# Block attention before two expert layers on one Trainium2 core: the first four attention steps laid out, paired and loaded in another way

## The chip, the core and the metric

The kernel runs on one core of a Trainium2 chip. The metric is the device time of one execution in microseconds (us); lower is better. Before the change three runs took 448.31, 448.86 and 450.56 us, median 448.86 us.

## What is computed

Three layers follow one another: causal attention with a decay over blocks of 64 positions (batch 2, 8 heads, 768 positions, head dimension 64), then `leaky(x @ w_in) @ w_out`, then a second expert layer with softmax and layer norm. Only the first is touched by the change:

```python
for b in range(nb):                                   # 12 blocks of 64 positions
    intra = np.einsum('bhic,bhjc->bhij', qb, kb) * Dmask[None]
    intra = np.einsum('bhij,bhjd->bhid', intra, vb)
    inter = np.einsum('bhid,bhde->bhie', qb * lam_pow[None], kv_state)
    out[:, :, sl] = intra + inter
    kb_dec = kb * rev_pow[None]
    kv_state = lam_block[None, :, None, None] * kv_state + np.einsum('bhsd,bhse->bhde', kb_dec, vb)
```

The result, 1536 tokens of 512 values, is the `x` of `h = x @ w_in` (512 to 2048), `g @ w_out` (2048 to 512) and so on.

## The kernel before

**Attention.** One step `s` (0 to 11) is one block of 64 positions, for both batches (`b`) and four pairs of heads (`pr`); the two heads of a pair (`h`) take the two halves of the 128 partitions. Each product is a matmul of a 64x64 stationary and a 64x64 moving operand, so it uses one quarter of the TensorE array: the half of the partitions that its operands lie on, and the half that its result goes to. Two products can lie beside each other in time where they use different quarters. A step has four groups of 16 matmuls (8 for each of the halves):

- `scores_mm` (L192): k times q. `scores_ev` (L198, VectorE) multiplies by the decay mask into `r`.
- `xs_mm` (L238): v times `r`, the part inside the block.
- `state_mm` (L206): decayed k times v. `scale_k` (L172) first multiplies k by its decay (ScalarE, four instructions); `state_ev` (L214) adds the old state, decayed by GpSimd (`decay_state`, L182), on VectorE.
- `xq_mm` (L250): state times scaled q (`scale_q`, L159, GpSimd), added in PSUM to the result of `xs_mm`.

`alone` issues a group by itself, `both` alternates two groups matmul by matmul. Each group is two batches, so `alone` is 32 instructions of 64x64 and `both` 64. The finished step is split into a high and a low part: `x_hi` (L287, ScalarE), then `x_lo` (L291, VectorE).

Steps 0 to 3 stand in a prologue written out by hand (L595 to L642). Steps 4 to 11 are sewn into the loop over the first expert layer. The two kinds have different layouts. From step 4 on, the operands of `xs_mm` and `state_mm` lie turned: the head that `q` has in the upper half has its `v` there too (`rows`, `jrows`). In steps 0 to 3 `v` and the third copy of k lie the other way round, so that `scores_mm` and `xq_mm` use the same two quarters and stand alone, and `xq_mm` writes with other rows of the array than `xs_mm`: a wait for the state's addition (L262) keeps them apart.

**Loads.** Nearly all go through the queue of SyncE (SPq) in program order, by `load` (L113). It adds a wait: a load is issued only when no more than `AHEAD` bytes, itself included, are under way. Beside this, the loads use eight counters in turn, so that a load also waits for the one eight before it. Step loads: `load_step` (L127), for one step two of 384 KB (q, k and k again, of one batch) and one of 256 KB (v). `load_kv` (L152) loads the turned operands of a later step in four of 128 KB, each for 64 partitions. `load_weights(n)` loads weight pair `n`, 512 KB for `IN` and 512 KB for `OUT`. The order is: table, step 0, pair 0, step 1, a copy of the mask, steps 2 and 3, pairs 1 to 3, step 4, pair 4, q and k of step 5, pair 5, and so on.

**Mask.** `scan(dfirst, 0, None)` makes the decay mask with four scans on VectorE; the turned mask `dmask` for steps 4 on is copied from it by two DMAs (L579).

**First expert layer.** The weights come as 64-bit words and are turned into two float parts: `words` (ScalarE, L336 and L337), `clamp`, `shift`, `join` (VectorE, L343, L353, L362), `high` (ScalarE, L392), `low` (VectorE, L411). `l1_mm((0, 0))` (L422) is the first product of the expert layer. It needs the high parts of all four steps. From there TensorE follows the order `l1_mm`, `l2_mm`, ..., 12 matmuls of 128x512 each (L422, L438).

## Time and profile before

| | |
|---|---|
| median of three runs | 448.86 us (448.31 to 450.56) |
| profiled execution, its own time | 449.68 us |
| span of its instructions | 447.9 us |
| TensorE busy | 434.0 us, 97% of the span |
| VectorE / ScalarE / GpSimd busy | 266.5 / 194.9 / 33.0 us |
| chain that ended last | TensorE 84%, DMA 8%, ScalarE 3%, VectorE 2% |

The profile's times are from the span's start; a TensorE instruction's time is its own, and neighbours overlap. [...] The DMA share is the mean busy share of 16 DMA engines. The landing time of a load runs from its issue to its completion.

### The profile page before, as it was taken

The page shows a single profiled execution, that of the slowest core. Times are in us where ns is not written, and L with a number is a line of the kernel's source. Part 1 is how long each engine was busy: PE and PEld are TensorE (multiplying, and loading weights), DVE is VectorE, ACT ScalarE, POOL GpSimd, SP SyncE. Part 2 cuts the span into 40 slices and gives each one's busy share as a digit, 9 for nine tenths or more (in the row PEclk, how much of TensorE's full clock was granted, in tenths as well). Part 3 has the DMA queues.
Part 4 walks back from the last instruction along what each step waited for, and adds up shares of the span by engine and source line. Part 5 has one row for each costly group of instructions (what it writes and reads, how often), then busy time and mean ns, then how long its engine had stood idle before and what let it go on. Part 6 is the DMA issues. An engine that isn't in the chain of part 4 may idle for free.

```text
span 447.9 us, 7951 instructions
## 1 busy us (share of the span) xinstructions
PE 434.0 (97%) x3252; PEld 358.2 (80%) x3252; DVE 266.5 (60%) x411; ACT 194.9 (44%) x326; POOL 33.0 (7%) x39
## 2 busy tenths in 40 slices
PE   6879899999999999999999999999999999999996
PEld 3868688888788888888888888888888888888886
DVE  3479898998932121211131788817779877777640
ACT  3477977868443232121233678622423322222221
POOL 0502022020102020100000000000000000000000
PEclk9699999999999999999999999999999999999999
DMA  7888875951303030100015653000112322222111
GB/s 264 253 282 265 288 273 153 320 194 50 94 0 97 1 95 1 48 0 1 1 23 184 225 198 122 1 0 5 44 34 58 98 72 74 74 75 74 58 48 47
DMA packets 23859, 46.98 MB, mean 105 GB/s; under 512 B 4368, under 2 KB 12176, under 8 KB 23312
## 3 DMA queue, kind: packets, MB, share of 16 engines
q1 hardware_dynamic: 21952, 44.92, 30.4%
q10 hardware_dynamic: 1872, 1.58, 1.2%
q8 instruction: 25, 0.41, 0.4%
q14 instruction: 10, 0.08, 0.1%
HBM read 37.95 MB, written 3.15 MB: 92 GB/s over the span
## 4 chain that ended last, share of the span: by engine, by line
PE 84%; DMA 8%; ACT 3%; DVE 2%; issue 1%; SPq 1%; ACTq 0%
PE acc L438 25%; PE hps L422 25%; PE acc L550 15%; PE aps L458 6%; PE hps L458 5%; PE acc L458 4%; DMA ldw<-in_att_dram 3%; DMA raww<-in_w_out_dram 2%; PE aps L242 1%; DMA qk<-in_att_dram 1%; PE aps L254 1%; PE acc L560 1%; DMA raww<-in_w_in_dram 1%; DMA kv<-in_vt_dram 1%; ACT x L336 1%; ACT raww L337 1%
## 5 line engine op out<-in xcount | busy, mean ns | idle before, releaser
L422 PE MATMUL hps<-xhi,wio 128*128 128x512 f32 x384 | 102.9, 390 | 3.1 <-ACT wio L392 2.4
L429 DVE TENSOR_TENSOR glo<-hps,ghi 128x512 fp32r<-128x512 f32 x48 | 33.2, 691 | 116.2 <-ACT ghi L428 115.8
L438 PE MATMUL acc<-ghi,wio 128*128 128x512 f32 x384 | 96.2, 393 | 0.1
L422 PEld LDWEIGHTS hps<-xhi,wio 128*128 128x128 f32 x384 | 71.7, 188 | 19.1 <-ACT wio L392 3.4
L438 PEld LDWEIGHTS acc<-ghi,wio 128*128 128x128 f32 x384 | 71.3, 188 | 15.6 <-ACT ghi L428 0.5
L425 ACT ACTIVATE hps<-hps 128x512 f32<-128x512 f32 x48 | 28.0, 583 | 116.6 <-PE hps L422 116.6
L550 PE MATMUL acc<-wb,ln 128*128 128x512 f32 (+1 forms) x312 | 67.6, 373 | 0.0
L550 PEld LDWEIGHTS acc<-wb,ln 128*128 128x128 f32 x312 | 55.3, 188 | 10.2
L422 PE MATMUL hps<-xlo,wio 128*128 128x512 f32 x192 | 51.4, 389 | 0.0
L438 PE MATMUL acc<-glo,wio 128*128 128x512 f32 x192 | 51.3, 389 | 0.0
L422 PEld LDWEIGHTS hps<-xlo,wio 128*128 128x128 f32 x192 | 36.0, 188 | 7.6
L438 PEld LDWEIGHTS acc<-glo,wio 128*128 128x128 f32 x192 | 36.0, 188 | 7.5
L353 DVE SCALAR_TENSOR_TENSOR raww<-x,raww 128x1024 uint32<-128x1024 uint32 (+1 forms) x27 | 31.2, 1154 | 0.5
L336 ACT ACTIVATE x<-raww 128x1024 f32<-128x1024 f32 (+1 forms) x27 | 27.7, 1027 | 7.5 <-DMA raww<-in_w_in_dram 5.2
L362 DVE SCALAR_TENSOR_TENSOR x<-x,raww 128x1024 uint32<-128x1024 uint32 (+1 forms) x27 | 29.6, 1096 | 0.8
L428 ACT CAST ghi<-hps 128x512 fp32r<-128x512 f32 x48 | 28.2, 587 | 1.5
L337 ACT ACTIVATE raww<-raww 128x1024 uint32<-128x1024 uint16 (+1 forms) x27 | 27.9, 1033 | 0.0
L491 POOL TENSOR_TENSOR small<-small,nhalf 128x1 f32<-128x1 f32 x12 | 6.6, 550 | 234.5 <-DVE small L490 234.5
L411 DVE TENSOR_TENSOR wio<-x,wio 128x1024 fp32r<-128x1024 f32 (+1 forms) x20 | 22.2, 1111 | 0.6 <-ACT wio L392 0.5
L553 ACT COPY osb<-acc 128x512 f32<-128x512 f32 (+1 forms) x13 | 7.2, 554 | 32.3 <-PE acc L550 19.2
L165 POOL TENSOR_TENSOR qk<-qk,qpow 128x512 f32<-128x512 f32 x8 | 11.3, 1406 | 135.4 <-PE hps L196 135.4
L458 PE MATMUL aps<-wa,xhi 128*128 128x512 f32 x80 | 19.8, 389 | 0.0
(96 smaller groups left out, 494.6 us busy)
## 6 DMA issues: line engine op xcount, KB each, us to landing
raww<-in_w_out_dram SPq DMA_DIRECT2D x23, 512.0 KB, 4.3
raww<-in_w_in_dram SPq DMA_DIRECT2D x16, 512.0 KB, 5.1
qk<-in_att_dram SPq DMA_DIRECT2D x8, 512.0 KB, 4.1
raww<-in_w_in_dram SPq DMA_DIRECT2D x4, 1024.0 KB, 4.8
lt<-e SPq DMA_DIRECT2D x124, 32.0 KB, 1.8
out_dram<-osb SPq DMA_DIRECT2D x11, 256.0 KB, 2.2
ldw<-in_att_dram SPq DMA_DIRECT2D x7, 384.0 KB, 5.1
kv<-in_att_dram SPq DMA_DIRECT2D x16, 128.0 KB, 3.2
```

What stands on the lines that cost most here:

```text
L336: act.activation(x, raw[:, :, 1].bitcast(F32), AF.Copy, scale=HI_SCALE)
L337: act.activation(raw[:, :, 0], raw.bitcast(U16)[:, :, 1], AF.Copy, scale=LO_SCALE)
L353: dve.scalar_tensor_tensor(raw[:, :, 0], x.bitcast(U32), 3, raw[:, :, 0], op0=ALU.logical_shift_left, op1=ALU.bitwise_or)
L362: dve.scalar_tensor_tensor(xu, xu, 0x80000000, raw[:, :, 0], op0=ALU.bitwise_and, op1=ALU.bitwise_or)
L411: dve.tensor_tensor(t[:, 1, halves], x[:, halves], t[:, 0, halves].bitcast(F32), op=ALU.subtract)
L422: pe.matmul(bank, w[:, s, k], x[b][:, k], start=(i == 0), stop=(i == len(terms) - 1))
L425: act.activation(bank, bank, AF.Prelu, alpha=0.01)
L428: act.copy(ghi, bank)
L429: dve.tensor_tensor(glo, bank, ghi.bitcast(F32), op=ALU.subtract)
L438: pe.matmul(acc[m], w[:, s, m], g, start=(f == 0 and first), stop=(f == NF - 1 and last))
L458: pe.matmul(bank, x[b][:, k, o : o + P], w2_t["a", k, half][:, s], start=(i == 0), stop=(i == len(terms) - 1),)
L550: pe.matmul(po[:, 0:n], x[:, k], w2_t["b", k][:, s, cols], start=(i == 0), stop=(i == len(terms) - 1))
```

## The change

Steps 0 to 3 take the layout of the later steps. Their q and k come in two loads of 256 KB, their v and the turned k in four loads of 128 KB with 64 partitions each. Those of step 0 are issued from ScalarE's queue, all others from SyncE's. `scores_mm` now uses the other two quarters than `xq_mm`, and the prologue alternates `xq_mm` of step s with `scores_mm` of step s + 1. In step 3 `xq_mm` comes first and `xs_mm` adds to it. The manual wait is gone. `dmask` is scanned directly, with no `dfirst` and no copy by DMA. `AHEAD` is 2 MB in place of 1.5 MB. The work on the weights in the prologue is in a slightly other order.

```diff
-AHEAD = 3 << 19
+AHEAD = 1 << 21
...
-    def load_step(s):
+    def load_turned(s, kj, v, queue=None):
+        queue = queue or sync
+        for h in range(2):
+            load(queue, out=v[rows(h)], in_=vt[s, HALF[h]])
+        for h in range(2):
+            load(queue, out=kj[rows(h)], in_=att[2 * s : 2 * s + 2, HALF[h], 2].rearrange("n p a b -> p n a b"))
+
+    def load_first_qk(s, queues):
         t = wp.tile([P, 2048], F32, tag="w", name="ldw")
-        qkk = t[:, 0:1536].rearrange("p (n c a b) -> p n c a b", n=NB, c=3, a=NPAIR)
-        v = t[:, 1536:2048].rearrange("p (n a b) -> p n a b", n=NB, a=NPAIR)
+        qk = qk_t[s] = t[:, 0:1024].rearrange("p (n c a b) -> p n c a b", n=NB, c=2, a=NPAIR)
+        kv = kv_t[s] = t[:, 1024:2048].rearrange("p (c n a b) -> p c n a b", c=2, n=NB, a=NPAIR)
         for b in range(NB):
-            load(act if s + b == 1 and s == 0 else sync, out=qkk[:, b], in_=att[2 * s + b])
-        load(sync, out=v, in_=vt[s])
+            load(queues[b], out=qk[:, b], in_=att[2 * s + b, :, 0:2])
...
-            pe.matmul(at(bank, jrows(s, h), b, pr), k[d, b, pr], q[d, b, pr], start=True, stop=True)
+            pe.matmul(at(bank, rows(h), b, pr), k[d, b, pr], q[d, b, pr], start=True, stop=True)
...
-            if s < NPRE and pr + b + h == 0:
-                tc.add_manual_dep(ins, added[s].name, SYNC, reason="another half of rows")
...
-    scan(dfirst, 0, None)
-    load_step(0)
+    load_first_qk(0, (act, sync))
+    load_first_kv(0, act)
     load_weights(0)
-    load_step(1)
-    for h in range(2):
-        load(sync, out=dmask[rows(h)], in_=dfirst[HALF[h]])
-    load_step(2)
-    load_step(3)
+    load_first_qk(1, (sync, sync))
+    load_first_kv(1)
...
     load_weights(1, IN)
     load_weights(1, OUT)
...
-    alone(scores_mm, 2, sb[0])
     state_ev(1, kb)
     decay_state(2, pool)
-    alone(xq_mm, 1, xb[1])
+    both(xq_mm, 1, xb[1], scores_mm, 2, sb[0])
     scores_ev(2, sb[0])
-    join(0)
     x_hi(1, xb[1])
+    high(0)
     both(xs_mm, 2, xb[0], state_mm, 2, kb)
     x_lo(1, xb[1])
     scale_q(3, pool)
     scale_k(3, act)
-    high(0)
-
-    alone(scores_mm, 3, sb[1])
     state_ev(2, kb)
     decay_state(3, pool)
-    alone(xq_mm, 2, xb[0])
+    low(0)
+    both(xq_mm, 2, xb[0], scores_mm, 3, sb[1])
     scores_ev(3, sb[1])
+    alone(xq_mm, 3, xb[1])
+    x_hi(2, xb[0])
     both(xs_mm, 3, xb[1], state_mm, 3, kb)
-    x_hi(2, xb[0])
-    state_ev(3, kb)
-    low(0)
-    alone(xq_mm, 3, xb[1])
     x_lo(2, xb[0])
     words(1, IN)
     x_hi(3, xb[1])
     bits(1, IN)
     x_lo(3, xb[1])
+    state_ev(3, kb)
     words(1, OUT)
```

The instructions of SyncE's queue around the end of the step loads, before. `DMAHW` with a number is one of the eight counters; `ldw` is a step's tile, `raww` a weight pair.

```order
L118 DMA ldw<-in_att_dram 128x768 [waits DMAHW7_49]
L118 DMA ldw<-in_att_dram 128x768 [waits DMAHW2_49]
L118 DMA ldw<-in_vt_dram 128x512 [waits DMAHW3_49]
L118 DMA raww<-in_w_in_dram 128x1024 [waits DMAHW4_49,DMAHW0_49]
L118 DMA raww<-in_w_out_dram 128x1024 [waits DMAHW6_49,DMAHW1_49]
L118 DMA raww<-in_w_in_dram 128x1024 [waits DMAHW7_49]
```

The same place with the change: step 3 (the first six rows), then pairs 1, 2 and the first half of 3.

```order
L109 DMA ldw<-in_att_dram 128x512 [waits DMAHW4_49]
L109 DMA ldw<-in_att_dram 128x512 [waits DMAHW5_49]
L109 DMA ldw<-in_vt_dram 64x512 [waits DMAHW6_49]
L109 DMA ldw<-in_vt_dram 64x512 [waits DMAHW7_49]
L109 DMA ldw<-in_att_dram 64x2x256 [waits DMAHW0_49]
L109 DMA ldw<-in_att_dram 64x2x256 [waits DMAHW1_49]
L109 DMA raww<-in_w_in_dram 128x1024 [waits DMAHW2_49]
L109 DMA raww<-in_w_out_dram 128x1024 [waits DMAHW3_49]
L109 DMA raww<-in_w_in_dram 128x1024 [waits DMAHW5_49,DMAHW4_49]
L109 DMA raww<-in_w_out_dram 128x1024 [waits DMAHW1_49]
L109 DMA raww<-in_w_in_dram 128x1024 [waits DMAHW6_49,DMAHW2_49]
```

Three loads of a step have become six, each with a wait on the counter in its turn, and the k that `scale_k` needs is last of the six; the first half of pair 1 stands behind it, and three more weight loads may be issued before it has landed.

ScalarE's instructions at the end of the prologue, before (`scale_k` of step 3, `high` of pair 0, `x_hi` of step 2, `words` of pair 1 IN, `x_hi` of step 3):

```order
L170 ACTIVATE ldw<-ldw,dfirst 128x2x64 [waits DMAHW6_49,DMAHW5_49]
L170 ACTIVATE ldw<-ldw,dfirst 128x2x64 x3
L392 CAST wio<-x 128x512 [waits DVE_49]
L289 CAST xhi_95<-acc_79 128x2x4x64 [waits PE_49]
L336 ACTIVATE x<-raww 128x512 [waits DMAHW0_49]
L337 ACTIVATE raww<-raww 128x512
L289 CAST xhi_95<-acc_80 128x2x4x64 [waits DVE_49,PE_49]
```

And with the change:

```order
L381 CAST wio<-x 128x512 [waits DVE_49]
L164 ACTIVATE ldw<-ldw,dmask 128x2x64 [waits DMAHW1_49,DMAHW0_49]
L164 ACTIVATE ldw<-ldw,dmask 128x2x64 x3
L278 CAST xhi_94<-acc_79 128x2x4x64 [waits PE_49]
L325 ACTIVATE x<-raww 128x512 [waits DMAHW2_49]
L326 ACTIVATE raww<-raww 128x512
L278 CAST xhi_94<-acc_80 128x2x4x64 [waits DVE_49,PE_49]
```

`high` of pair 0 has moved ahead of `scale_k` of step 3; `words` of pair 1 IN stands ahead of the last `x_hi` in both.

## Rows read from the trace of the kernel before

**Rows 1.** Busy times by stretch; columns: stretch, length, engines, PEclk, DMA share, GB/s.

```profile
64.00:96.00 32.00, 32.00 (x379) 26.50 (x378) 29.20 (x31) 26.02 (x36) 4.17 (x3) 1.00 0.65 212
```

**Rows 2.** The chain that ended last: start us, us, what.

```profile
9.15 6.41 DMA ldw<-in_att_dram
...
41.49 4.61 DMA raww<-in_w_out_dram
```

**Rows 3.** Instructions in order of time, TensorE: start, us, what [idle before <-releaser].

```profile
24.22 0.73 PE L254 MATMUL acc<-qs,state 64*64 64x64 f32 x17 [0.88 <-DVE state L236]
26.09 0.68 PE L254 MATMUL acc<-qs,state 64*64 64x64 f32 x15 [1.14 <-issue]
27.44 2.11 PE L422 MATMUL hps<-xhi,wio 128*128 128x512 f32 x8 [0.68 <-ACT xhi L289]
...
50.44 1.20 PE L422 MATMUL hps<-xhi,wio 128*128 128x512 f32 x4 [1.92 <-ACT wio L392]
```

**Rows 4.** The same for ScalarE.

```profile
22.94 0.67 ACT L336 ACTIVATE x<-raww 128x512 f32<-128x512 f32 x1
23.50 0.66 ACT L337 ACTIVATE raww<-raww 128x512 uint32<-128x512 uint16 x1
26.81 0.59 ACT L289 CAST xhi<-acc 128x512 fp32r<-128x512 f32 x1 [2.65 <-PE acc L254]
...
46.12 1.17 ACT L336 ACTIVATE x<-raww 128x1024 f32<-128x1024 f32 x1 [0.74 <-DMA raww<-in_w_out_dram]
```

**Rows 5.** The same for VectorE.

```profile
23.47 0.69 DVE L236 TENSOR_TENSOR state<-aps,sd 128x512 f32<-128x512 f32 x1 [1.35 <-PE aps L210]
...
27.42 0.69 DVE L293 TENSOR_TENSOR xlo<-acc,xhi 128x512 fp32r<-128x512 f32 x1 [0.94 <-ACT xhi L289]
```

**Rows 6.** Busy times by stretch, as rows 1, in the load-bound part.

```profile
2.00:22.00 20.00, 15.57 (x386) 12.49 (x386) 9.51 (x20) 7.51 (x20) 6.03 (x6) 0.83 0.86 281
22.00:50.50 28.50, 23.79 (x227) 19.00 (x223) 23.89 (x38) 21.55 (x35) 3.61 (x3) 1.00 0.87 287
...
32.00:36.00 4.00, 3.90 (x18) 2.88 (x17) 3.84 (x7) 2.58 (x6) 0.00 (x0) 1.00 0.84 236
44.00:48.00 4.00, 4.00 (x19) 3.30 (x19) 3.85 (x6) 2.50 (x3) 0.00 (x0) 1.00 1.02 354
```

**Rows 7.** Loads issued at 7.92, 16.51 and 22.27 us: KB each, us to landing.

```profile
dmask<-dfirst SPq DMA_DIRECT2D x1, 64.0 KB, 6.7
...
ldw<-in_vt_dram SPq DMA_DIRECT2D x1, 256.0 KB, 4.5
...
raww<-in_w_out_dram SPq DMA_DIRECT2D x1, 512.0 KB, 6.2
```

**Rows 8.** Instructions in order of time, SyncE's queue.

```profile
28.50 0.39 SPq L118 DMA_DIRECT2D qk<-in_att_dram x1
30.57 1.37 SPq L118 DMA_DIRECT2D kv<-in_att_dram x2
31.98 1.24 SPq L118 DMA_DIRECT2D kv<-in_vt_dram x2
```

**Rows 9.** TensorE, first and last rows of two alternated pairs of groups (64 matmuls each).

```profile
7.53 0.27 PE L242 MATMUL acc<-r,ldw 64*64 64x64 f32 x2 [0.79 <-DVE r L204]
...
8.47 0.23 PE L210 MATMUL aps<-ldw 64*64 64x64 f32 x2
...
14.13 0.37 PE L242 MATMUL acc<-r,ldw 64*64 64x64 f32 x2 [0.79 <-DVE r L204]
...
15.80 0.32 PE L210 MATMUL aps<-ldw 64*64 64x64 f32 x2
```

**Rows 10.** Busy times by stretch, as rows 1: granted clock and idle TensorE.

```profile
11.50:12.00 0.50, 0.00 (x0) 0.00 (x0) 0.00 (x0) 0.00 (x0) 0.00 (x0) 0.96 1.07 385
12.00:12.50 0.50, 0.28 (x6) 0.28 (x7) 0.00 (x0) 0.21 (x1) 0.16 (x1) 0.50 1.12 418
...
18.50:19.00 0.50, 0.50 (x22) 0.50 (x22) 0.50 (x2) 0.00 (x0) 0.42 (x1) 0.71 0.87 322
```

More of the change, by code (lines that the diff above doesn't have):

```diff
@@ L175, in scale_k @@
             return
-        kj, last = ld[s][KJ], decay(s)
+        kj, last = ld[s][KJ], dmask
         if eng is act:
@@ L202, in scores_ev @@
         for src, dst in parts(bank, r_t[s]):
[L203 removed]
+            mask = dmask if len(src.shape) == 3 else dmask.unsqueeze(1).to_broadcast(SHAPE)
             dve.tensor_tensor(dst, src, mask, op=ALU.mult)
@@ L231, in state_ev @@
                     op1=ALU.add,
-                ).ins
-                added.setdefault(s, ins)
+                )
             return
         for src, dst, old in parts(bank, s_t[s + 1], sd_t[s]):
-            added[s] = dve.tensor_tensor(dst, src, old, op=ALU.add).ins
+            dve.tensor_tensor(dst, src, old, op=ALU.add)
     def xs_mm(s, bank, b, pr):
         for h in range(2):
-            j = jrows(s, h)
+            j = rows(h)
             pe.matmul(
@@ L245, in xs_mm @@
                 r_t[s][j, b, pr],
-                start=(s == 0 or pr + b == 0),
-                stop=(s == 0),
+                start=(s == 0 or s != NPRE - 1 and pr + b == 0),
+                stop=(s == 0 or s == NPRE - 1 and pr + b == NPAIR + NB - 2),
             )
@@ L257, in xq_mm @@
                 qs_t[s][d, b, pr],
-                start=False,
-                stop=(pr + b == NPAIR + NB - 2),
-            ).ins
-            if s < NPRE and pr + b + h == 0:
-                tc.add_manual_dep(ins, added[s].name, SYNC, reason="another half of rows")
+                start=(s == NPRE - 1 and pr + b == 0),
+                stop=(s != NPRE - 1 and pr + b == NPAIR + NB - 2),
+            )
     def each_pair(*groups):
@@ L574, in fused_kernel @@
     load(sync, out=tabs, in_=tab)
-    scan(dfirst, 0, None)
-    load_step(0)
+    load_first_qk(0, (act, sync))
+    load_first_kv(0, act)
     load_weights(0)
-    load_step(1)
-    for h in range(2):
-        load(sync, out=dmask[rows(h)], in_=dfirst[HALF[h]])
-    load_step(2)
-    load_step(3)
+    load_first_qk(1, (sync, sync))
+    load_first_kv(1)
+    load_first_qk(2, (sync, sync))
+    load_first_kv(2)
+    load_first_qk(3, (sync, sync))
+    load_first_kv(3)
     load_weights(1, IN)
@@ L606, in fused_kernel @@
     decay_state(1, pool)
+    bits(0)
+    x_lo(0, xb[0])
     alone(scores_mm, 1, sb[1])
-    bits(0)
     scores_ev(1, sb[1])
-    x_lo(0, xb[0])
+    join(0)
     both(xs_mm, 1, xb[1], state_mm, 1, kb)
```

32 lines of the change are left out of this document (12 added, 20 removed).

## The prediction

> **What bounds the kernel now.** I read the busy times by stretch first: from 64 us on TensorE is busy in 32.00 of 32 us [rows 1], and the stretches behind it look the same up to the last few microseconds. Nothing in the change touches that part, so only the beginning can move, and every microsecond by which TensorE's unbroken work starts earlier is a microsecond of the result. The chain that ended last says what sets the beginning: between 9.15 and 46.10 us it is a row of loads, the first and the last of which stand in [rows 2]. The order in time shows where this reaches TensorE. `l1_mm((0, 0))` starts at 27.44, as soon as the last `x_hi` is done (26.81 + 0.59), and after a gap of 1.92 us TensorE goes on at 50.44 for good [rows 3, 4]. Two times are to be forecast, then: the start at 27.44 and the resumption at 50.44. VectorE is busy 23.89 of the 28.50 us between 22 and 50.5, most of its idle time being at the beginning, so behind `l1_mm` it has little to give back [rows 6].
>
> **The step loads.** Up to the landing of step 3's `v` (issued at 16.51, landing 4.5 later, at 21.0 [rows 7]) the queue moves table, four steps and half of pair 0, 132 + 4096 + 512 KB or 4.85 MB, and a mask copy whose first 64 KB took 6.7 us to land [rows 7]. The copy falls away. The six loads of a step cost SyncE's queue two issues of about 0.39 and four of 1.37 / 2 and 1.24 / 2 [rows 8], 3.4 us per step. The bytes cost 1.05 MB at the 281 GB/s of this part [rows 6], 3.7 us. The larger, 3.7, is the pace I take; it also fits the counters, since eight loads of 175 KB under way (1.43 MB) at some 5 us each are 286 GB/s. So in this part 2 MB are never under way: the eight counters close first. Step 1's second load has to wait for the first load of step 0, about 4.4 us; three steps on, the last is issued at 4.4 + 3 x 3.7 = 15.5 and, with 4.5 to 5 us to landing, is there at about 20.2, 0.8 us before the old one. The bounds: at 354 GB/s, the best long stretch, the 4.85 MB, which begin to move at 2 us, are there at 2 + 13.7 + about 1 = 17; at 236, the stretch in which a later step's loads by halves move, at 2 + 20.6 = 22.6 [rows 6].
>
> **The end of the prologue.** Behind the last k come `scale_k` (1.3 us), the second half of the last alternated groups (0.6), and `x_hi`. Two groups alternated run from 7.53 to 8.70, 1.17 us, and at the lower clock level from 14.13 to 16.12, 2.0 us [rows 9], so that a pair costs what one group alone does; the two new pairs save about 1.1 us each on TensorE, and the removed manual wait a further 0.9, the idle time before `xq_mm` at 24.22 [rows 3]. Before, 6.4 us lay between the landing of step 3 and `l1_mm`; with the change some 3.5. But the last `x_hi` stands behind `words` of pair 1 IN on ScalarE, as the order rows show, and that waits for a load which is now issued right behind the last k, with three more 512 KB loads allowed beside it. A load with two others under way took 6.2 us [rows 7]; 512 KB more at 354 GB/s make it 7.7. Issued at 16, pair 1 IN lands between 21.7 (in turn, 20.2 + 1.5) and 23.7. I take 23.0, nearer to the late end, because the measured load shared too. `words` and `x_hi` need 1.75 us from there (two starts 0.56 apart, as at 22.94 and 23.50, then 0.59 [rows 4]): **`l1_mm` at 24.75, 2.7 us earlier**. TensorE's own idle 1.14 before 26.09 ("issue", no releaser [rows 3]) is hidden even if it recurs, as `words` covers it.
>
> **From there to the resumption.** The work is as before, 23.0 us, with two corrections on VectorE and ScalarE. `state_ev` of step 3, which stood before the last `x_lo` at 23.47, now follows it: 0.6 us more on VectorE between `l1_mm` and the `high` that ends the gap [rows 5]. The wait of 0.74 for pair 5 OUT at 46.12 [rows 4] goes if that load comes in time. They cancel. For that, pair 5 OUT must land 2.7 earlier, at 43.4. Behind pair 1 IN 6.36 MB are loaded (pairs 1 OUT to 5, step 4, q and k of step 5, a constant). Before they took from 22.3 to 46.1, 267 GB/s at about 0.87 of the engines' share [rows 6]; 2 MB under way, four weight loads in place of three, should fill the idle share: 267 / 0.87 = 307 GB/s, and 23.0 + 20.7 = 43.7. So the load costs back 0.3 of the 2.7 at worst, and I count 2.55.
>
> **What costs nothing.** The scans are the same four on VectorE. ScalarE now issues five loads, the last one after the table has landed; its first work waits for pair 0, whose load now is issued two microseconds earlier. k of step 0 comes later than the old one, but step 1's loads end later still.
>
> **Sum.** 449.68 - 2.55 = 447.1 for the profiled execution. Its time is 0.8 above the median of 448.86; against the median it is 446.3.
>
> [...] Each set of halves is priced by the stretch of 236 GB/s against 354 [rows 6]. [...]
>
> **Rivals.**
>
> *Halves are slow throughout.* All step loads at 236 GB/s: 22.6 for the last k, 1.7 more for pair 1 IN (512 KB at the 307 of the next part), `l1_mm` at 26.05, a gain of 1.4: 447.5. For it: the stretch at 32 to 36. Against it: only half of a step's bytes comes by halves.
>
> *More bytes under way bring no more per second.* The queue stays at 267 GB/s behind pair 1 IN: 23.0 + 23.8 = 46.8 for pair 5 OUT, and TensorE resumes at 50.4 to 51.1, gain zero: 448.9 to 449.5. This is the case in which the change does not do what it says. For it: 1.5 MB already gave 354 GB/s at a share of 1.02 [rows 6]. Against it: the share over the whole part was 0.87.
>
> *The step loads fill the queue.* 354 GB/s [rows 6], with some loss in between: last k below 19, pair 1 IN at 21.5, `l1_mm` at 23.4, gain 4.0: 444.9. Pair 5 OUT has to keep up, at 330 GB/s or more.
>
> *Slower: the clock stays low.* The granted clock fell to 0.50 at 12 us, after TensorE had been idle, and rose between 18.5 and 19, in a stretch of work that began at 14.13 [rows 9, 10]. With fewer microseconds of work in the same time it may not rise in the prologue. Then each pair of groups costs 2.0 [rows 9], the last ones end at 26.0, `l1_mm` starts at 26.7 and, if the rise takes as long again, runs its first 4.5 us at half speed, which loses 2.25: 28.95, 1.5 later than before, 450.4. It decides against the change once the low level reaches more than 1.5 us into `l1_mm`, and by over 0.5% once more than 6 us. Against it: between 23.5 and 27.4 TensorE was mostly idle (its two pieces there are 0.73 and 0.68 us [rows 3]) and the clock held.
>
> **How the numbers follow.** Forecast 0.45, slow halves 0.18, no more bandwidth 0.12, full queue 0.15, low clock 0.10. A measurement of this kernel tells about 0.5% or 2.24 us from no change. The forecast's 2.55 lies just beyond; of its 0.45 I give 0.33 to faster and 0.12 to the same, and with the full queue's 0.15 faster has 0.48. Slower takes 0.08 of the low clock. The rest, 0.44, is the same. The range reaches from 444.3, below the full queue, to 449.6, which takes in the case without more bandwidth and leaves out most of the low clock.
>
> **What would show it.** Right: `l1_mm` starting between 24 and 25.5, released by `x_hi` behind `words`, the load of pair 1 IN landing 1 to 3 us after the last k; GB/s above 300 between 22 and 44; the gap before TensorE's resumption still near 1.9. The halves: 230 to 240 GB/s in 4 to 20 us. No bandwidth: a wait of more than 1 us of `words` for pair 5, landings of weight loads of 7 us in place of 5. The clock: 0.50 at the start of `l1_mm`. My forecast is wrong altogether if the resumption is not the end of the wait, that is if TensorE idles again between 50 and 100 us.

## The result, and the profile after

The changed kernel takes 451.21 us in the median (448.65 to 452.48, 20 runs). The kernel before, run beside it, takes 447.61 (445.46 to 450.94, 20 runs). The ratio is 1.0063, with a 95% interval of 1.0045 to 1.0081: slower by over half a per cent. Forecast were 446.3 us and "faster". 451.21 lies outside the range, above its upper end of 449.6.

The profiled execution took 451.08 us with a span of 449.2. From the page: busy time of TensorE, and the shares of the chain that ended last.

```profile
PE 434.5 (97%) x3252; PEld 358.4 (80%) x3252; DVE 267.6 (60%) x411; ACT 194.8 (43%) x326; POOL 33.9 (8%) x39
...
PE 88%; DVE 4%; ACT 3%; issue 2%; ACTq 0%
```

The loads have gone from the chain, where they had 8%. "issue" has come in. TensorE in order of time shows where (L411 was L422, L427 was L438; compare [rows 3]):

```profile
26.34 0.36 PE L204 MATMUL aps<-ldw 64*64 64x64 f32 x1 [2.62 <-issue]
27.72 3.78 PE L411 MATMUL hps<-xhi,wio 128*128 128x512 f32 x8 [0.58 <-ACT xhi L278]
...
35.45 1.98 PE L427 MATMUL acc<-ghi,wio 128*128 128x512 f32 x8
...
51.70 1.20 PE L411 MATMUL hps<-xhi,wio 128*128 128x512 f32 x4 [1.16 <-ACT wio L381]
```

TensorE stands still for 2.62 us in the middle of step 3's last alternated groups, some 17 products of 64x64 before `l1_mm`, and waits for nothing that the profile shows. `l1_mm` starts at 27.72, where 24.75 was forecast and 27.44 was the start before. Its first eight products take 3.78 us, before 2.11. ScalarE's rows say that the loads are not to blame ([rows 4] before):

```profile
21.11 1.28 ACT L164 ACTIVATE ldw<-ldw,dmask 128x128 f32<-128x128 f32 x4 [1.43 <-DMA ldw<-in_att_dram]
...
22.76 0.69 ACT L325 ACTIVATE x<-raww 128x512 f32<-128x512 f32 x1
23.34 0.68 ACT L326 ACTIVATE raww<-raww 128x512 uint32<-128x512 uint16 x1
27.09 0.59 ACT L278 CAST xhi<-acc 128x512 fp32r<-128x512 f32 x1 [3.07 <-PE acc L233]
```

`words` of pair 1 IN runs at 22.76 without a wait, so its load was there by then. ScalarE is ready for the last `x_hi` at 24.0 and waits 3.07 us for TensorE. The stretches (columns as [rows 1]) give the loads' pace and the clock:

```profile
4.00:20.00 16.00, 10.50 (x295) 8.72 (x297) 9.47 (x18) 7.33 (x16) 6.25 (x5) 0.79 0.95 288
...
22.00:44.00 22.00, 18.80 (x179) 15.23 (x175) 16.52 (x29) 15.92 (x29) 2.78 (x3) 0.84 0.99 338
...
25.50:26.00 0.50, 0.00 (x0) 0.00 (x0) 0.00 (x0) 0.00 (x0) 0.00 (x0) 0.52 1.01 401
...
32.00:32.50 0.50, 0.50 (x3) 0.37 (x3) 0.50 (x2) 0.50 (x2) 0.00 (x0) 0.65 1.10 258
32.50:33.00 0.50, 0.50 (x4) 0.42 (x3) 0.41 (x2) 0.50 (x3) 0.00 (x0) 1.00 1.05 297
```

From 22 to 44 us 338 GB/s are moved, before 272 in the same stretch (287 up to 50.5 us [rows 6]). The granted clock (PEclk, as a share of full speed), full again since 19 us, falls to 0.50 at 25.5, during the stand-still, and comes back at about 32.3. Those are 4.6 us of `l1_mm` and what follows at half speed.

**What the 2.62 us are.** Among the DMA queues q8 carries instructions. The same 25 packets, 0.41 MB, run in both kernels, each 16 KB. One of them starts in the half microsecond from 23.5, at 23.99:

```profile
q8 instruction: 1, 0.02, 11.5%
```

It took 0.92 us (11.5% of 16 engines' 0.5 us), and 2.35 us after its start TensorE goes on. Before, it was the same: a packet starts at 23.73, and TensorE goes on at 26.09, 2.36 us later, after the "issue" of 1.14 [rows 3]. In all eleven profiles with such a stand-still near `l1_mm`, those of the experiments included, it ends 2.2 to 3.0 us after the start of a packet. In the kernel before TensorE had come to this place at 24.95 (26.09 - 1.14), in the changed one at 23.72. Against this profile the prologue did become faster by 1.2 us there, and TensorE stood still until 2.35 us after the packet's start. That it waits there for the instructions in the packet is the author's reading, and rests on these times: no view names what it waits for. The packet's own 0.92 us were over 1.43 us before TensorE went on, and in the kernel before its 1.09 us (6.8% of 16 us) were over at 24.82, just before TensorE stopped. (A second profile of the kernel before, `g1_before_again` below, passes the same place at 22.89 without standing still.)

### The profile page after: what moved, and what is told of

Read it like the earlier page. It is cut to its first block, busy times and chain, and to the rows that moved or that the text cites. A ratio compares the mean times of both kernels' runs of the same rounds, so it can differ in the third digit from the quotient of the medians.

```text
span 449.2 us, 7967 instructions
## 1 busy us (share of the span) xinstructions
PE 434.5 (97%) x3252; PEld 358.4 (80%) x3252; DVE 267.6 (60%) x411; ACT 194.8 (43%) x326; POOL 33.9 (8%) x39
## 4 chain that ended last, share of the span: by engine, by line
PE 88%; DVE 4%; ACT 3%; issue 2%; ACTq 0%
PE hps L411 27%; PE acc L427 26%; PE acc L539 15%; PE aps L447 6%; PE hps L447 5%; PE acc L447 4%; PE aps L233 1%; PE aps L245 1%; PE aps L204 1%; DVE wio L400 1%; ACT x L325 1%; ACT raww L326 1%; DVE r L198 1%; DVE raww L342 1%; PE hps L190 1%
## 5 line engine op out<-in xcount | busy, mean ns | idle before, releaser
L411 PE MATMUL hps<-xhi,wio 128*128 128x512 f32 x384 | 104.6, 395 | 2.2 <-ACT wio L381 1.7
L427 PE MATMUL acc<-ghi,wio 128*128 128x512 f32 x384 | 96.1, 392 | 0.0
L411 PEld LDWEIGHTS hps<-xhi,wio 128*128 128x128 f32 x384 | 72.7, 191 | 18.6 <-ACT wio L381 2.7
L427 PEld LDWEIGHTS acc<-ghi,wio 128*128 128x128 f32 x384 | 71.4, 188 | 15.2
L411 PE MATMUL hps<-xlo,wio 128*128 128x512 f32 x192 | 51.9, 392 | 0.0
L427 PE MATMUL acc<-glo,wio 128*128 128x512 f32 x192 | 51.3, 389 | 0.0
L411 PEld LDWEIGHTS hps<-xlo,wio 128*128 128x128 f32 x192 | 36.6, 190 | 7.8
L427 PEld LDWEIGHTS acc<-glo,wio 128*128 128x128 f32 x192 | 36.0, 188 | 7.5
L342 DVE SCALAR_TENSOR_TENSOR raww<-x,raww 128x1024 uint32<-128x1024 uint32 (+1 forms) x27 | 32.1, 1188 | 0.5
L381 ACT CAST wio<-x 128x1024 fp32r<-128x1024 f32 (+1 forms) x20 | 17.6, 878 | 6.0 <-DVE x L351 5.9
```

Of the source, the lines that this page charges most:

```text
L342: dve.scalar_tensor_tensor(raw[:, :, 0], x.bitcast(U32), 3, raw[:, :, 0], op0=ALU.logical_shift_left, op1=ALU.bitwise_or)
L411: pe.matmul(bank, w[:, s, k], x[b][:, k], start=(i == 0), stop=(i == len(terms) - 1))
L427: pe.matmul(acc[m], w[:, s, m], g, start=(f == 0 and first), stop=(f == NF - 1 and last))
```

## The experiments

Two names are used in the expectations. Q: the bytes under way hold up the instruction packet. S: the packets come at a pace of their own, whatever else loads.

**Is it regular, and is it tied to the instructions?** `i1_after_again` is the changed kernel and `g1_before_again` the kernel before, each profiled once more.

> The changed kernel, unchanged, profiled once more, since the kernel before showed TensorE's stand-still before the last products of step 3 in one profile (1.14 us) and not in the other. Theory (in the changed kernel the instruction packet is regularly late): a stand-still of 2 to 3.5 us some 17 products before the feed-forward's first, which start at 27.2 to 28.5, at the low clock. Rival (the first profile was an odd one): no stand-still above 1.2 us, the first products at 24.6 to 26.0; then the loss of 3 us in the median has another cause.

```profile
26.91 0.36 PE L204 MATMUL aps<-ldw 64*64 64x64 f32 x1 [3.25 <-issue]
28.29 3.78 PE L411 MATMUL hps<-xhi,wio 128*128 128x512 f32 x8 [0.58 <-ACT xhi L278]
```

Regular: 3.25 us, at the same product, with `l1_mm` again at the low clock; 451.53 us. `e3_shift24` puts 24 more products ahead, in the warm-up:

```diff
-NWARM = 12
+NWARM = 36
-        pe.matmul(acc[0], c1.to_broadcast([P, P]), c1.to_broadcast([P, 512]), start=True, stop=True)
+        pe.matmul(acc[0][:, 0:170], c1.to_broadcast([P, P]), c1.to_broadcast([P, 170]), start=True, stop=True)
```

> The changed kernel with its 12 warm-up matmuls of 512 columns split into 36 of 170, so that TensorE's program has 48 instructions more ahead of everything, in the same time. Theory of the instruction count (common to Q and S): the idle time 'issue' moves to a place 24 matmuls earlier, some 38 matmuls before the expert layer; it ends 0.3 to 1 us earlier and the expert layer starts at about 27.2. Rival T (the idle time is tied to a moment or to a load, not to an instruction): it stays at about 14 matmuls from the end and at 23.7 us.

```profile
28.14 0.37 PE L204 MATMUL aps<-ldw 64*64 64x64 f32 x1 [3.58 <-issue]
30.16 3.78 PE L411 MATMUL hps<-xhi,wio 128*128 128x512 f32 x8 [0.58 <-ACT xhi L278]
```

The stand-still moves to some 40 products before `l1_mm`, about 24 earlier in the sequence: it belongs to a place in TensorE's instructions, not to an operand. The earlier place did not help. It grew to 3.58 us, and the kernel took 451.99 us, ratio 1.0084 (1.0047 to 1.0122).

**Do the bytes under way make it?** `e1_ahead_1m5` sets the limit back to 1.5 MB in the changed kernel, `e2_before_2m` raises it to 2 MB in the kernel before, and `e5_ahead_768k` lowers it to 768 KB in the changed one.

```diff
-AHEAD = 1 << 21
+AHEAD = 3 << 19
```

> The changed kernel with 1.5 MB of loads under way in place of 2 MB, nothing else. In the changed kernel TensorE stood still for 2.62 us at 23.72 (releaser 'issue') in the last alternated groups, with some 14 matmuls left before the expert layer; the kernel before stood still for 1.14 us with 15 left. Theory Q (more loads under way hold up the packets of TensorE's own instructions): the idle time shrinks to 1.2 to 1.8 us, the expert layer starts near 26.5, and 1 to 2 us of the loss come back (ratio to before 1.002 to 1.004). Theory S (the instructions take their time whatever the loads, and TensorE uses them up faster since its groups alternate): the idle time stays at 2.3 to 2.9, the expert layer starts near 27.7, the ratio stays at 1.005 to 1.008 or rises a little, as the weights come later.

> The kernel before with 2 MB of loads under way, nothing else. Theory Q: TensorE's idle time 'issue' before the expert layer grows from 1.14 to 2 us or more, the expert layer starts 1 us or more later, ratio 1.002 to 1.004. Theory S: the idle time stays at 0.8 to 1.4 us, the expert layer starts at 27.2 to 27.7, ratio 0.997 to 1.001 (pair 5 comes earlier, the 1.92 us gap at 50 loses up to 0.7 us).

> The changed kernel with 768 KB of loads under way in place of 2 MB. The loads get slower, so the whole is slower; looked at is how long TensorE's instructions take. In the changed kernel the packet of instructions was read at 23.8 us and TensorE went on at 26.34, some 5.7 us after it had begun the block before. Theory Q (loads under way hold up the instruction packets): TensorE stands still for under 0.5 us in the last groups, or not at all, and the clock stays at 1.00 at the expert layer's start unless the loads themselves leave TensorE idle. Theory S (the packets take their time whatever the loads): where TensorE gets through the last block in under 5 us it still stands still until some 5.5 us have passed. Time: ratio 1.01 to 1.03 in both.

`g2_hold_loads` and, the same once more, `i2_hold_again` let nothing but instructions load from about 23 us until the last `x_hi`:

```diff
-    load_weights(1, OUT)
-    load_weights(2)
...
     x_hi(3, xb[1])
+    hold.append(nc.cur_bb.bb.instructions[-1])
+    load_weights(1, OUT)
+    load_weights(2)
...
+        if len(hold) == 1:
+            tc.add_manual_dep(ins, hold[0].name, SYNC, reason="hold")
```

> The changed kernel with every load behind the first half of weight pair 1 held back until the last high half of the attention output is written (about 27 us), so that nothing but instruction packets is under way on the DMA engines from about 23 us on. Theory Q (the bytes under way hold up TensorE's instruction packet): the stand-still before the last products of step 3 shrinks from 2.62 to at most 1.2 us, and the first products of the feed-forward start at 26.3 or before. Rival S (a block of instructions takes its time whatever else is loading): the stand-still stays at 2.3 to 2.9 and they start at 27.4 to 28.0. The end comes later than in the changed kernel under both, by 3 to 10 us, since weight pairs 2 to 4 come late.

> The changed kernel with the loads behind the first half of pair 1 held back until about 24 us, profiled once more: in the first profile the stand-still was 0.23 us and the feed-forward started at 24.84, as forecast for the changed kernel. Theory Q (bytes under way hold up the instruction packet): again no stand-still over 0.6 us, start at 24.6 to 25.3. Rival (chance): a stand-still of 1 to 3 us and a start after 25.8.

`i3_limit_1m_from_pair1` keeps 2 MB for the steps and allows 1 MB from pair 1 on (the "as before" in its expectation is a slip: the limit before was 1.5 MB).

```diff
-            if ahead > AHEAD:
+            if ahead > limit[0]:
...
     load_weights(1, IN)
+    limit[0] = 1 << 20
```

> The changed kernel with 2 MB under way only up to the loads of step 3, and 1 MB, as before, from weight pair 1 on: the layout, the alternation and the early loads of the prologue stay. Theory Q: half the bytes stand before the packet that TensorE waits for at 23 to 26 us, the stand-still falls to 0.5 to 1.5 us and the feed-forward starts at 25.0 to 26.5; weight pairs 2 to 5 come later again, so that the resumption is near 48.5 to 50 and the time 448 to 450, ratio 0.999 to 1.004. Rival S: the stand-still stays at 2 to 3, start 27.2 to 28, ratio 1.006 to 1.010.

First `g2_hold_loads`: TensorE's rows, and the stretch ahead of them, in which nothing loads.

```profile
23.71 0.27 PE L207 MATMUL aps<-ldw 64*64 64x64 f32 x1 [0.23 <-issue]
24.84 2.11 PE L414 MATMUL hps<-xhi,wio 128*128 128x512 f32 x8 [0.64 <-ACT xhi L281]
```

```profile
22.00:24.00 2.00, 1.77 (x82) 1.53 (x77) 1.53 (x4) 1.89 (x4) 0.75 (x1) 1.00 0.00 0
```

Then `i2_hold_again`, and `i3_limit_1m_from_pair1`.

```profile
24.72 0.27 PE L207 MATMUL aps<-ldw 64*64 64x64 f32 x1 [1.06 <-issue]
25.86 2.11 PE L414 MATMUL hps<-xhi,wio 128*128 128x512 f32 x8 [0.64 <-ACT xhi L281]
```

```profile
25.04 0.27 PE L204 MATMUL aps<-ldw 64*64 64x64 f32 x1 [1.03 <-issue]
26.18 2.11 PE L411 MATMUL hps<-xhi,wio 128*128 128x512 f32 x8 [0.64 <-ACT xhi L278]
...
54.23 2.08 PE L411 MATMUL hps<-xhi,wio 128*128 128x512 f32 x4 [6.33 <-ACT wio L381]
```

With no other loads, `l1_mm` starts at 24.84 and 25.86; forecast were 24.75. All kernels with the changed prologue that came to this place, at 23.5 to 24.0 us:

| kernel | limit near 23 us | stand-still | TensorE goes on | `l1_mm` | clock there |
|---|---|---|---|---|---|
| changed / again | 2 MB | 2.62 / 3.25 | 26.34 / 26.91 | 27.72 / 28.29 | 0.50 |
| `e6_apart` (below) | 2 MB | 2.11 | 26.02 | 27.16 | falls at 27.5 |
| `e1_ahead_1m5` | 1.5 MB | 1.36 | 25.04 | 26.18 | 1.00 |
| `i3_limit_1m_from_pair1` | 1 MB | 1.03 | 25.04 | 26.18 | 1.00 |
| hold, again / first | none | 1.06 / 0.23 | 24.72 / 23.71 | 25.86 / 24.84 | 1.00 |

With the changed prologue Q is borne out: the fewer bytes, the earlier TensorE goes on, by up to 3 us; S would have left 2.3 to 2.9. But each row is one profile, that of `e1_ahead_1m5` is its fastest execution (448.38, median 450.88), the second hold missed its expectation, and `e2_before_2m` seems to speak against: the old sequence with 2 MB stood still 1.03 us, no more than with 1.5, and took 448.90 us, ratio 1.0001 (0.9971 to 1.0030).

```profile
25.00 0.68 PE L254 MATMUL acc<-qs,state 64*64 64x64 f32 x15 [1.03 <-issue]
```

By the same reading the stand-still depends on two things, though: on when the packet comes, and on how long TensorE needs for its products up to that place. The packets tell the two apart. From one such place to the next TensorE issues 127 products. From the first of these 127 to the start of the packet that by this reading belongs behind the last one it is:

| limit near 23 us | profiles | us |
|---|---|---|
| 2 MB | 12, among them `e2_before_2m` with 3.00 | 2.36 to 5.27 |
| 1.5 MB | 4: the kernel before twice, `e1_ahead_1m5`, `e7_late_1m5` | 1.37 to 3.02 |
| 1 MB / 768 KB | `i3_limit_1m_from_pair1` / `e5_ahead_768k` | 1.09 / 0.89 |
| none | hold, again / first | 1.16 / 0.90 |

(The first of the 127 is counted back; six profiles show a short stop there, too.) So bytes under way do hold up the packet, with 2 MB by 1.2 to 4.4 us against the holds; between 2 and 1.5 MB the profiles overlap. `e2_before_2m` stood still so little because TensorE needed 4.15 us for its 127 products (19.82 to 23.97); the changed kernel needs 3.06 (20.66 to 23.72). S is right in this part: the faster TensorE gets through, the longer it stands.

In `e5_ahead_768k` TensorE waited for loads and what hangs on them (up to 7.5 us at once), and no stand-still near these places is marked "issue": 495.88 us, ratio 1.1058 (1.1008 to 1.1109), far off what was expected, so that it says nothing of Q. Nor does a smaller limit pay. `e1_ahead_1m5` takes 450.88, ratio 1.0051 (1.0025 to 1.0077), so the 1 to 2 us that Q was to give back did not come. `i3_limit_1m_from_pair1` takes 456.37, ratio 1.0178 (1.0149 to 1.0208): weight pair 4 is so late that TensorE waits 6.33 us. The hold costs 453.22 and 453.77 us in one run each.

The counts agree with the reading. 25 packets for the 3252 products of an execution are one for 130; from 281 us on 129 to 131 products run in the changed kernel from one packet's start to the next; from one place to the next it is 127, and 24 products more ahead moved the place by about 24. No view names the engine whose instructions a packet holds.

**Is the stand-still the loss?** `e4_state_late` keeps the whole change and moves step 3's state products (nothing needs them before step 4) behind the first `l1_mm`. Then 32 fewer products stand ahead of `l1_mm`, and the place of the stand-still comes behind its first products.

```diff
-    both(xs_mm, 3, xb[1], state_mm, 3, kb)
+    alone(xs_mm, 3, xb[1])
...
-    state_ev(3, kb)
...
     l1_mm((0, 0), hps[0])
+    alone(state_mm, 3, kb)
...
     join(1, OUT)
+    state_ev(3, kb)
```

> The changed kernel with the last state products (step 3, 32 matmuls) issued after the first product of the expert layer, and their addition on VectorE later; the same matmuls in all. The place at which TensorE ran out of instructions then lies behind the first 12 matmuls of the expert layer. Theories Q and S: no idle 'issue' before the expert layer, which starts at 24.5 to 25.2 at the high clock level; the resumption comes at 48 to 49.5, ratio 0.992 to 0.997. Rival C (the low clock and the late first step lose the time, not the stand-still): the expert layer starts after 26.5 or at 0.50, ratio over 1.002.

```profile
24.64 2.11 PE L411 MATMUL hps<-xhi,wio 128*128 128x512 f32 x8 [1.12 <-ACT xhi L278]
...
28.34 1.03 PE L204 MATMUL aps<-ldw 64*64 64x64 f32 x29 [0.42 <-issue]
...
48.41 1.20 PE L411 MATMUL hps<-xhi,wio 128*128 128x512 f32 x4 [1.15 <-ACT wio L381]
```

`l1_mm` starts at 24.64 at the full clock, and TensorE resumes at 48.41; 47.9 was forecast (50.44 - 2.55). The time is 448.06 us, ratio 0.9996 (0.9975 to 1.0016). So the stand-still and the clock behind it are the loss of the change, about 3 us, and nearly all of it is the late start: from `l1_mm` to TensorE's resumption it is 23.77 us here and 23.98 in the changed kernel, where the 32 products lie ahead. Yet without it the kernel is no faster than before.

`e6_apart` takes the alternation of `xq_mm` and `scores_mm` out of the changed kernel, `e8_late_apart` out of `e4_state_late`.

```diff
-    both(xq_mm, 1, xb[1], scores_mm, 2, sb[0])
+    alone(scores_mm, 2, sb[0])
+    alone(xq_mm, 1, xb[1])
...
-    both(xq_mm, 2, xb[0], scores_mm, 3, sb[1])
+    alone(scores_mm, 3, sb[1])
+    alone(xq_mm, 2, xb[0])
```

> The changed kernel with xq of steps 1 and 2 and the scores of steps 2 and 3 in groups of their own again, same layout and loads. TensorE is then some 1 us later in each of the two places. If its instructions are what it waits for in the end, the stand-still gets shorter by about as much (2.62 to 1.0 to 1.8 us) and ends at the same time; fewer runs drop to the low clock before the expert layer; ratio 1.002 to 1.005, better than the changed kernel. If the alternation is worth what the prediction gave it (theory A), the expert layer starts 1 us or more later and the ratio rises to 1.008 or more.

> The kernel with the last state products after the expert layer's first product, and the groups of xq and scores apart again. If alternation shortens the prologue once instructions are no longer waited for, this is 0.5 to 1.5 us slower than with alternation, ratio 1.001 to 1.004, with the expert layer's start at 25.2 to 26. If the loads set the end of the prologue, the start stays at 24.6 to 25 and the ratio at 0.997 to 1.001.

1.0060 (1.0037 to 1.0083) apart and 1.0063 alternated; 0.9983 (0.9963 to 1.0004) apart and 0.9996 alternated. The alternation brings nothing that can be measured in the time, with the stand-still or without. On TensorE it does bring something: from its first product to the next group a pair takes 1.22 us alternated (20.41 to 21.63 in the changed kernel), 1.72 apart (20.95 to 22.67 in `e8_late_apart`) and 2.15 in the kernel before (20.02 to 22.17). In the changed kernel the 64 products of the pair, on all four quarters, take hardly more than the 32 of the next group, alone on two: 1.10 us (21.63 to 22.73). In `e8_late_apart` `l1_mm` starts at 25.39, 0.75 later than in `e4_state_late`, as was expected if alternation shortens the prologue; but the clock came back at 19.05 us in this profile and at 13.90 in that one, so this difference is not the alternation's alone.

```profile
25.39 2.12 PE L411 MATMUL hps<-xhi,wio 128*128 128x512 f32 x8 [0.69 <-ACT xhi L278]
...
48.52 1.21 PE L411 MATMUL hps<-xhi,wio 128*128 128x512 f32 x4 [1.15 <-ACT wio L381]
```

`e8_late_apart`, 448.14 us, has the lowest ratio of all versions, and is not shown to be faster than before.

**Where does the rest of the gain go?** `g1_before_again` had an answer in it.

> The kernel before, unchanged, profiled once more. The execution on which the forecast was built took 449.68 us, above the median of its own later runs (447.6 to 448.6), and TensorE took up the feed-forward products for good at 50.44 us in it. From that point to the end every profile so far took 397.4 to 397.6 us, so a run of 447.8 has to have taken them up at about 48.6. Theory (the base was a slow execution: at least 1.5 us of the forecast gain was measured against a run that is not the usual one): here the resumption lies at 48.3 to 49.3, with TensorE's stand-still before the last products of step 3 present (about 1 us). Rival (the base was typical and the difference lies around the span): the resumption lies at 50.2 to 50.7 again.

```profile
24.20 2.11 PE L422 MATMUL hps<-xhi,wio 128*128 128x512 f32 x8 [0.69 <-ACT xhi L289]
...
48.83 1.25 PE L422 MATMUL hps<-xhi,wio 128*128 128x512 f32 x4 [3.21 <-ACT wio L392]
```

```profile
49.50:50.00 0.50, 0.50 (x4) 0.41 (x3) 0.50 (x1) 0.50 (x3) 0.00 (x0) 0.84 0.93 344
50.00:53.00 3.00, 3.00 (x9) 2.22 (x7) 2.66 (x3) 2.11 (x2) 0.00 (x0) 0.50 0.90 306
```

Here the kernel before had no stand-still, and its `l1_mm` began 3.24 us earlier than in [rows 3]. It resumed only 1.61 earlier, after a wait of 3.21 us in place of 1.92, ran some 3.5 us at 0.50, and ended with a span of 447.8: 0.1 less. An early start is given back in the kernel before, too. The resumption was as expected, the end was not: 399.0 us from there, where the thirteen profiled executions without a fall of the clock or a later wait need 397.4 to 397.6.

How early `l1_mm` comes is partly the execution, then, and not the kernel: here TensorE waited 1.34 us for the step loads of step 1 and the clock was back at 15.70, against 2.84 us and 18.79 in the profile of [rows 3]. In the seven profiles of the changed prologue with 2 MB in which TensorE had no such stand-still in the last microseconds ahead of `l1_mm`, it starts at 23.99 to 25.73. That the new prologue gets there sooner than the old one's 24.20 is not shown.

The rows of VectorE between 24 and 48 us hardly have a gap, so the next kernels take work from it or put it in another order. `g3_pool_clamp` is `e8_late_apart` with seven clamps on GpSimd (its expectation counts eight) and GpSimd's work on step 4 issued ahead of the last of them. `g4_pool_clamp_words` also takes pair 1 earlier on ScalarE. `i4_words4_early`, without the clamps, has ScalarE take pair 4 earlier.

```diff
-        dve.tensor_scalar(x, x, HI_MAX, -HI_MAX, op0=ALU.min, op1=ALU.max)
+        eng = pool if 1 < n <= NPRE + 1 or n == 1 and halves == OUT else dve
+        eng.tensor_scalar(x, x, HI_MAX, -HI_MAX, op0=ALU.min, op1=ALU.max)
```

> The changed kernel with step 3's state products behind the first feed-forward products, product groups apart, and besides the clamps of weight pairs 1 (second half) to 5 on GpSimd instead of VectorE. Theory (from the first feed-forward products to the resumption VectorE sets the pace, so in the version with the state products moved nothing more came of the early start): VectorE loses 8 clamps of 0.42 to 0.69 us, some 3.5 us, of its work between 24 and 48 us, GpSimd takes about 1.1 us for each beside it, the resumption moves from 48.5 to about 46.5, and the kernel ends at 445.5 to 447, ratio to before 0.993 to 0.997. Rival (ScalarE or the loads are right behind VectorE): the resumption moves by under 0.7 and the ratio is 0.997 to 1.000.

> As the one before, and ScalarE takes the first half of weight pair 1 before the attention output of steps 2 and 3, and the scaling of step 3's keys behind it (their product comes later anyway). VectorE can start on pair 1 about 0.5 to 1 us sooner. If the theory of VectorE's pace holds, the resumption moves by another 0.5 to 1 us against the kernel without this (about 45.8) and the ratio to before is 0.991 to 0.996. Rival (the load of pair 1 lands too late, or ScalarE is the bound): no difference to the kernel without this beyond 0.3 us, or up to 0.7 slower.

> The changed kernel with step 3's state products behind the first feed-forward products, groups apart, and weight pair 4's words on ScalarE ahead of the last parts of pair 3 and of the split of the third product, so that the conversion of pair 4 ends sooner. In the version without this (profile: resumption at 48.52 after a wait of 1.15 us for pair 4) TensorE is busy without a break from 28 to 47.4. Theory: the wait goes, the resumption lies at 47.4 to 47.8, the time at 446.9 to 447.6, ratio 0.994 to 0.9985. Rival (pair 4's load lands too late for that, or the split of the third product is delayed): TensorE waits earlier, the resumption stays at 48.3 to 49.5, ratio 0.998 to 1.003.

All three missed: 450.87, ratio 1.0050 (1.0022 to 1.0079); 451.81, ratio 1.0074 (1.0048 to 1.0100); 448.17, ratio 0.9990 (0.9966 to 1.0014). VectorE's rows of `g3_pool_clamp` give the reason, then GpSimd's:

```profile
44.53 2.08 DVE L343 SCALAR_TENSOR_TENSOR raww<-x,raww 128x1024 uint32<-128x1024 uint32 x1
46.65 1.94 DVE L352 SCALAR_TENSOR_TENSOR x<-x,raww 128x1024 uint32<-128x1024 uint32 x1
```

```profile
44.02 1.52 POOL L184 TENSOR_TENSOR sd<-state,qpow 128x512 f32<-128x512 f32 x1
45.50 2.01 POOL L333 TENSOR_SCALAR x<-x 128x1024 f32<-128x1024 f32 x1
```

In `e8_late_apart`, with GpSimd idle, the same `shift` and `join` of a whole pair take 1.22 and 1.23 us:

```profile
44.85 1.22 DVE L342 SCALAR_TENSOR_TENSOR raww<-x,raww 128x1024 uint32<-128x1024 uint32 x1
46.10 1.23 DVE L351 SCALAR_TENSOR_TENSOR x<-x,raww 128x1024 uint32<-128x1024 uint32 x1
```

The clamps came off VectorE and slowed what was left. TensorE resumed at 49.77 after 2.71 us of waiting, and the clock fell to 0.50 from 50.5 to 53.9. In `i4_words4_early` the same happens with GpSimd's work on step 4:

```profile
39.52 1.02 DVE L332 TENSOR_SCALAR x<-x 128x512 f32<-128x512 f32 x1
40.64 1.37 DVE L342 SCALAR_TENSOR_TENSOR raww<-x,raww 128x512 uint32<-128x512 uint32 x1
```

```profile
38.95 1.30 POOL L159 TENSOR_TENSOR qk<-qk,qpow 128x512 f32<-128x512 f32 x1 [15.31 <-PE hps L190]
40.22 1.24 POOL L184 TENSOR_TENSOR sd<-state,qpow 128x512 f32<-128x512 f32 x1
```

Elsewhere these two take 0.42 and 0.69. In `e8_late_apart` the same work of GpSimd already stretches a `low` from 0.68 to 1.28 us and a clamp to 0.68, so this is not shown to be the whole reason why `i4_words4_early` missed. The rows show it with two inputs (`shift`, 1.37 instead of 0.69 us) and with one (the clamp, 1.02 instead of 0.42).

`j1_state3_behind_pair4` is `e8_late_apart` with `state_ev` of step 3 behind pair 4's `join`, and pair 4's `high` ahead of a split. `j2_pool_after_pair4` also holds GpSimd back until pair 4 is through.

```diff
-    state_ev(3, kb)
...
             join(4)
+            join4 = nc.cur_bb.bb.instructions[-1]
+            state_ev(3, kb)
...
                 scale_q(NPRE, pool)
+                tc.add_manual_dep(nc.cur_bb.bb.instructions[-1], join4.name, SYNC, reason="after pair 4")
```

> The changed kernel with step 3's state products behind the first feed-forward products, groups apart, and now VectorE's sum of step 3's state (0.69 us) behind the last operation on weight pair 4; ScalarE casts pair 4's high words before it splits the fourth product. Moving ScalarE's words forward brought nothing (resumption 48.59), VectorE being occupied without a break. Theory (VectorE's conversion of pair 4 sets the resumption): 48.5 moves to 47.6 to 48.0, the wait before it falls to 0.3 to 0.7 us, the time to 447.1 to 447.6, ratio to before 0.995 to 0.999. Rival (something else takes its place, or the time is given back at steps 4 and later): resumption at 48.3 or later, or the same end as without it; ratio 0.998 to 1.001.

> As the one before, and GpSimd's scaling of step 4's queries waits until VectorE is through with pair 4. In the profiles VectorE's operations took longer while GpSimd ran beside them (the clamp 1.02 instead of 0.42 us, the shift 1.37 instead of 0.69, near 40 us, and 2.08 and 1.94 instead of 1.22 with GpSimd's clamps near 45). Theory (the two engines slow each other): VectorE gains another 0.6 to 1.2 us before the resumption, which lies at 47.0 to 47.5, with no wait for pair 4 left; time 446.5 to 447.2, ratio 0.993 to 0.998, unless pair 5 is then late by the same amount. Rival (no such contention, or it only moves to pair 5): within 0.3 us of the one before.

First TensorE in `j1_state3_behind_pair4`, then in `j2_pool_after_pair4`, then VectorE there.

```profile
46.89 1.19 PE L411 MATMUL hps<-xhi,wio 128*128 128x512 f32 x4 [0.91 <-ACT wio L381]
...
61.12 1.19 PE L411 MATMUL hps<-xhi,wio 128*128 128x512 f32 x4 [0.50 <-ACT wio L381]
```

```profile
48.00 1.19 PE L411 MATMUL hps<-xhi,wio 128*128 128x512 f32 x4 [0.31 <-ACT wio L381]
...
50.84 1.20 PE L411 MATMUL hps<-xhi,wio 128*128 128x512 f32 x4 [0.72 <-DVE wio L400]
...
62.99 1.21 PE L411 MATMUL hps<-xhi,wio 128*128 128x512 f32 x4 [0.51 <-ACT wio L381]
```

```profile
47.33 1.45 DVE L332 TENSOR_SCALAR x<-x 128x1024 f32<-128x1024 f32 x1
48.70 2.08 DVE L400 TENSOR_TENSOR wio<-x,wio 128x1024 fp32r<-128x1024 f32 x1
```

From `l1_mm` to the resumption `e8_late_apart` takes 23.13 us (25.39 to 48.52), `j1_state3_behind_pair4` 22.90 (23.99 to 46.89), `j2_pool_after_pair4` 22.27 (25.73 to 48.00). The 22.27 is the shortest of all profiles, so VectorE does have a part in the resumption; 22.90 alone would not show it, since `e1_ahead_1m5` took 22.85. That TensorE resumed earlier than the 47.6 expected in `j1_state3_behind_pair4` comes mostly from its `l1_mm`, 1.40 earlier. And new waits of 0.5 to 0.7 us follow at 51 to 63 us, and from the resumption to the end it is 398.5 and 399.4 us instead of 397.5. Likely what VectorE is spared for pair 4 is missing at pairs 5 and 6, and GpSimd's contention only moves, as the last two rows show it (0.69 and 1.22 us in `e8_late_apart`); the waits alone are 0.5 and 1.2 us of the 1.0 and 1.9 lost. 448.65 us, ratio 0.9992 (0.9970 to 1.0014), and 448.64, ratio 1.0004 (0.9975 to 1.0032).

Last, `e7_late_1m5` is `e4_state_late` with 1.5 MB.

> The kernel with the last state products after the expert layer's first product, and 1.5 MB under way. With the stand-still out of the way the loads should show: if 2 MB help (as predicted), this is 0.5 to 2 us slower than the same with 2 MB, ratio 1.001 to 1.005, with a longer wait for pair 5 near 45 us. If more bytes under way bring nothing, the ratio is the same as with 2 MB, 0.997 to 1.001.

452.35 us, ratio 1.0071 (1.0036 to 1.0105). Once the stand-still is out of the way the 2 MB are worth some 4 us, twice the most that was expected. Its runs fall into two groups, three at 447.27 to 449.51 and eight at 451.14 to 453.20. The profiled one, 449.13, is of the first: TensorE resumes there at 49.83 after 1.82 us. What the others lose is not shown. It is not simply the clock: their mean granted clocks lie between 0.979 and 0.996, and the one with 0.996, as much as the profiled execution had, took 452.67.

## Why the prediction was wrong

- **The step that failed** is "TensorE's own idle 1.14 before 26.09 ("issue", no releaser [rows 3]) is hidden even if it recurs, as `words` covers it." It is no fixed idle time that moves along with the work. It ends 2.2 to 3.0 us after an instruction packet starts (eleven profiles), and the faster TensorE gets there the longer it stands: 2.62 and 3.25 us. Against the profile before, 1.18 of the 1.48 us more come from TensorE (3.06 us for the 127 products in place of 4.24) and some 0.3 from the packet (3.33 us behind their first in place of 3.02). `words` covered nothing, since it was over at 24.0. Not even the old 1.14 would have been hidden: after stand-stills of 1.03 and 1.36 us `l1_mm` starts at 26.18. Of the 2.97 us by which `l1_mm` missed 24.75, the stand-still is nearly all: in one of the two holds, with 0.23 us left of it, it starts at 24.84. Without it the path of the forecast holds: in `e4_state_late` the last `x_hi` follows `words` at 24.01 without a wait, and `l1_mm` starts at 24.64.
- **The clock** came on top. The rival of the low clock came near with its time (450.4 us) by luck. It was right that `l1_mm` begins at half speed, and wrong in the mechanism and the price: the prologue is not too sparse for the clock to rise, but the clock falls anew in the stand-still (to 0.50 at 25.5, after 1.00 from 19 us on), and 4.6 us at half speed cost less than the 2.25 us given. From `l1_mm` to the resumption it is 23.4 to 24.0 us in the five profiles that start at 0.50 or fall to it there, and 23.0 and 22.85 in the kernel before and `e1_ahead_1m5` at 1.00, so some 0.4 to 1.1 us. The argument against it, that the clock held between 23.5 and 27.4 with TensorE mostly idle, rested on a stand-still of 1.14 us.
- **"Every microsecond by which TensorE's unbroken work starts earlier is a microsecond of the result"** holds from the resumption on (397.4 to 397.6 us) while the clock stays up and VectorE keeps pace. The sentence that it "has little to give back" was right, and its consequence was not drawn: an earlier `l1_mm` meets a longer wait for pair 4. `g1_before_again` started 3.24 us earlier and ended 0.1 earlier.
- **The base.** 449.68 less 2.55 makes 447.1 for a profiled run; `e4_state_late`, in which the early start came about, was profiled at 447.96. But the kernel before has a median of 447.61 to 448.69 over the sets of runs here. Its 449.68 was longer than any of these medians, and a gain worked out against it was mostly the way back to the usual. The prediction took off 0.8 for this in its last step, but its 27.44 and 50.44, from which the gain is worked out, stayed those of that execution; `l1_mm` came at 24.20 in the other profile of this kernel.
- **The loads were nearly right.** The last k was there at 21.1 (forecast 20.2, not earlier than before), pair 1 IN before 22.76 (23.0). 338 GB/s behind 22 us (307), so pair 5 comes without a wait. Halves are not slow: 288 GB/s between 4 and 20 us, before 292 in the same stretch, not 230 to 240.
- **The alternation** was "about 1.1 us each" on TensorE. The second pair gains 0.9 against the old groups (2.15 to 1.22) and 0.5 against groups apart in the new layout, and the kernel with groups apart is no slower. In the changed kernel TensorE only reaches the stand-still sooner; without it the stretch behind `l1_mm` likely gives the gain back.

## What to carry to other kernels

Idle time marked "issue" is a resource, too: see whether it sits at a fixed place in the instruction sequence and whether an instruction packet is read near it, before counting it as hidden or as moving along. If it does, put long products or work that nothing waits for at that place, not the last short products before a critical one (in `e4_state_late` 0.42 us stood at that place, and `l1_mm` began at 24.64). And before a gain at the start is counted in full, profile the old kernel twice, and ask which engine paces the stretch behind it.
